# A fused Fourier-mixing and two-product kernel: the second product runs three rounds behind the first, and the transform's pieces get two places in a round

## The chip, the cores and the metric

One core of a Trainium2 chip runs the whole program. TensorE (PE in the profile, with its weight loads as PEld), VectorE (DVE), ScalarE (ACT), GpSimd (POOL) and SyncE (SP, which issues the transfers here) each work through a list of their own in order and wait for each other by semaphores. The metric is the device time in microseconds (us) of one execution of the program.

## The reference

Eight sequences of 3008 tokens and 256 features pass through a real Fourier transform along the sequence, a complex 256x256 mix with a bias and a soft threshold, and the inverse transform. The result, 24064 rows of 256, goes through a block of two products with 2048 hidden features, whose nonlinearity is the square of a relu.

```python
X = np.fft.rfft(x, axis=1); Xr, Xi = X.real, X.imag
Yr = Xr @ w_r - Xi @ w_i + b_r
Yi = Xr @ w_i + Xi @ w_r + b_i
Yr, Yi = (np.sign(v) * np.maximum(np.abs(v) - 0.01, 0.0) for v in (Yr, Yi))
y = np.fft.irfft(Yr + 1j * Yi, n=3008, axis=1)      # x of the second part, 24064 x 256
h = np.maximum(y @ w_in, 0.0)                       # 24064 x 2048
out = h * h @ w_out                                 # 24064 x 256
```

## The kernel before

A start-up part loads the weights, splits them into a high and a low fp32r part and transforms the first sequences. After it the program is a loop of rounds, written out by hand (L904): 47 chunks of 512 tokens, eight rounds a chunk, 376 rounds and the two that empty the pipe. Round r does the following for its chunk.

- The **first product** (`mm1`, tile `ph`, 12 matmuls of 512 columns) for 256 hidden features. ScalarE takes it out of PSUM (relu L863, square L864), VectorE makes three sums of it (`sums`, L869 to L871).
- The hidden tile of the round before is split: ScalarE copies the high part `gh` (L916), VectorE subtracts the low part `gl` (L927).
- The **second product** (`mm2`, tile `po`, 14 matmuls with `gh` and 7 with `gl`, 256 columns each) for the hidden tile of `LAG` = 2 rounds before. It adds up in four PSUM banks over eight rounds; in the round of a chunk's last one `put_together` reads them (one ScalarE copy, seven VectorE operations L890 to L896) and stores the result. This round is called the chunk end below.

Between these the transform of later sequences is threaded in, one piece at a time. Each piece is a few matmuls into one bank of `ps_f`, a pool of two PSUM banks that are given out in turn: a piece takes the bank that the piece but one before it had, and waits until that one has been read.

- Piece A (`psa`, 6 matmuls of 256 columns), first step of the transform of a group of columns; ScalarE copies it out (`eva`). Before it come `f` (VectorE), `fh` (ScalarE), `fl` (VectorE).
- A pair B: `psb` (8 small matmuls; ScalarE reads it into `x`, VectorE sums, both split it to `xh`, `xl`); two rounds later the mix `psm`, 18 matmuls into two banks at once, which VectorE reads one after the other (`e`, L233 and L234) and thresholds (`t`, L727, and `e`, L728); then ScalarE turns it (`z`), both split it (`zh`, `zl`), and `psc` (3 matmuls of 512 columns) goes back; ScalarE copies it out (`evc`).
- Piece D (`psd`, 8 small matmuls), last step; ScalarE copies half of it (`dv`, L784), VectorE combines it with the other half (`dx`, L275 and L276), which frees the bank; then it is split into `xt`, the operand of the first product.

Where a step stands is set by a place in the round: `load`, `p1` (pieces behind the first product), `e` (ScalarE, behind the square), `p2` (behind the second product), `a` and `v` (ScalarE and VectorE, last in the round). `PAIR_WORK` and the others are guesses of PE, ScalarE and VectorE time, by which `spread` chooses the rounds of pieces A and D; `pair_rounds` fixes those of the pairs. In this text rounds count from 0 and a chunk end before has r mod 8 = 1.

Of the kernel before, what the change touches and what calls it, by code (L numbers as in the profile page):

```python
# [20 lines left out]
NPAIR = NR // 2  # L21
# [128 lines left out]
def fft_mix_moe(ctx: ExitStack, tc: tile.TileContext, xp, xu, w_r, w_i, b_r, b_i,  # L150
# [473 lines left out]

    rounds = pair_rounds(B)
    last = nch * NU
    plan = {}
    works = np.zeros((last + 64, 3))
# [14 lines left out]
    A_WORK = ((-3, 0, 0, .8), (-2, 0, .6, .7), (0, .7, .6, 0))  # L643
    D_WORK = ((0, .9, .4, .8), (1, 0, .7, .7))
    SUM_WORK = (0, 0, .3, 2.9)

    def plan_a(b, i, r):
# [38 lines left out]
        at(r, "p1", points)  # L686
        at(r, "e", out)

    def plan_b(b, i, r):
# [82 lines left out]
    def plan_d(i, r, later):  # L772
# [16 lines left out]

        at(r - 1, "load", load)  # L790
        at(r, "p1", points)
        at(r, "e", take)
        at(r, "v", unfolded)
        for n, piece in enumerate(pieces(i)):
            q = later if n else r + 1
            at(q, "a", lambda piece=piece: high_x(piece, s["x"]))
            at(q, "v", lambda piece=piece: low_x(piece, s["x"]))

    for b, rs in rounds.items():
        for r in rs:  # L800
            note(r, *PAIR_WORK)
    for c in range(nch):
        works[c * NU + NU + 1] += SUM_WORK[1:]

    mixes = {r + 2 for rs in rounds.values() for r in rs}
    def spread(n, lo, hi, work, apart):

        best = [{} for _ in range(n)]
        for i in range(n):
            for r in range(lo, hi + 1):  # L810
                if r in mixes:
                    continue
                cost = sum(max(0., float(np.sum(works[r + d] + w))) ** 2 - float(np.sum(works[r + d])) ** 2
                           for d, *w in work)
                before = min(((c, q) for q, (c, _) in best[i - 1].items() if q <= r - apart),
                             default=None) if i else (0., ())
                if before is not None:
                    best[i][r] = before[0] + cost, (best[i - 1][before[1]][1] if i else ()) + (r,)
        got = min(best[-1].values())[1]
        for r in got:  # L820
            note(r, *work)
        return got

    begin = 3
    for b in range(2, B):
        end = rounds[b][0] - 3
        got = spread(len(GROUPS), begin, end, A_WORK, 2)
        begin = max(got[-1] + 2, rounds[b][0] - 12)
        for i, r in enumerate(got):
            plan_a(b, i, r)  # L830
# [6 lines left out]
    free = 2  # L837
    for c in range(1, nch):
        own = [i for i in range(len(flat)) if begins[i] // CH == c]
        parts = [[i for i in own if flat[i][0] == b] for b in sorted({flat[i][0] for i in own})]  # L840
        for n, part in enumerate(parts):
            b = flat[part[0]][0]
            lo = max(NU * (c - 1), free, rounds[b][-1] + 9 if b else 2)
# [128 lines left out]
```

## Time and profile before

| what | value |
|---|---|
| median of 3 runs (lowest to highest) | 2706.86 us (2706.52 to 2708.56) |
| the profiled execution | 2706.33 us, of it span of the trace 2704.2 us |
| PE, PEld busy | 2580.7 us (95%), 2288.4 us (85%) |
| DVE, ACT busy | 2112.6 us (78%), 1982.9 us (73%) |
| granted TensorE clock, mean | 0.99 |
| DMA, mean over the span | 61 GB/s |

Busy time is the time that an engine had an instruction in work, as a share of the span. A matmul's end is modelled: a matmul of 512 columns is shown 0.39 us long while the next one starts 0.23 us after it, so a wait of TensorE shows shorter in the busy time than from one start to the next. The first matmul of round 2 starts at 155.13 us.

### The profile page before, as it was taken

How to read it: one execution, taken by the hardware profiler on the slowest of the kernel's cores; microseconds unless marked ns; L12 is line 12 of the kernel's file. 1: busy time of each engine (PE TensorE's matmuls, PEld its weight loads, DVE VectorE, ACT ScalarE, POOL GpSimd, SP SyncE). 2: the span in 40 equal slices, each digit the busy share in tenths (PEclk: the TensorE clock that was granted, in tenths of full speed). 3: DMA queues.
4: the chain of work that ended last, by engine and by line, in shares of the span. 5: the costliest groups of instructions: out<-in, count | busy, mean ns of one | idle time of the engine just before them, and what ended most of it. 6: DMA issues, size and time to landing. Idle time of an engine off the chain costs nothing.

```text
span 2704.2 us, 41768 instructions
## 1 busy us (share of the span) xinstructions
PE 2580.7 (95%) x16496; PEld 2288.4 (85%) x16496; DVE 2112.6 (78%) x3155; ACT 1982.9 (73%) x2764; POOL 48.2 (2%) x57
## 2 busy tenths in 40 slices
PE   7889999999999999999999999999999999999998
PEld 4578888888888889888888888888888998888887
DVE  5777887877788878877888788887887778777776
ACT  4667776767777777777787777877777777776766
POOL 1500000000000000000000000000000000000000
PEclk8999999999999999999999999999999999999999
DMA  8522222211112111121112111211111111001000
GB/s 261 182 67 65 65 65 69 65 50 60 56 57 69 57 57 56 60 65 46 56 60 68 54 57 53 75 53 51 57 56 48 38 39 51 31 24 35 16 27 16
DMA packets 113092, 164.57 MB, mean 61 GB/s; under 512 B 9584, under 2 KB 63074, under 8 KB 112706
## 3 DMA queue, kind: packets, MB, share of 16 engines
q1 hardware_dynamic: 112898, 161.91, 19.3%
q8 instruction: 131, 2.15, 0.3%
q14 instruction: 63, 0.52, 0.1%
HBM read 86.90 MB, written 74.97 MB: 60 GB/s over the span
## 4 chain that ended last, share of the span: by engine, by line
PE 72%; ACT 11%; DVE 7%; issue 7%; DMA 1%; SPq 0%; DVEq 0%; ACTq 0%
PE po L878 17%; PE ph L184 10%; PE ph L182 10%; PE ph L183 10%; PE po L882 9%; ACT gh L916 4%; ACT g L863 4%; PE psd L268 3%; PE psm L184 2%; PE psm L182 2%; PE psm L183 2%; PE psb L219 1%; DVE gl L927 1%; PE psc L182 1%; ACT x L223 1%
## 5 line engine op out<-in xcount | busy, mean ns | idle before, releaser
L927 DVE TENSOR_TENSOR gl<-g,gh 128x1792 fp32r<-128x1792 f32 x376 | 761.2, 2025 | 144.2 <-ACT gh L916 144.1
L863 ACT ACTIVATE g<-ph 128x512 f32<-128x512 f32 x752 | 408.4, 595 | 592.0 <-PE ph L184 590.9
L878 PE MATMUL po<-gh,wo 128*128 128x256 f32 x5264 | 703.6, 284 | 29.2 <-DVE o L891 17.9
L878 PEld LDWEIGHTS po<-gh,wo 128*128 128x128 f32 x5264 | 657.9, 189 | 57.5 <-DVE o L895 16.7
L916 ACT CAST gh<-g 128x1792 fp32r<-128x1792 f32 x376 | 636.2, 1692 | 0.2 <-DVE g L871 0.2
L182 PE MATMUL ph<-xt,wi 128*128 128x512 f32 x1504 | 592.7, 394 | 10.1 <-DVE dx L276 8.8
L184 PE MATMUL ph<-xt,wi 128*128 128x512 f32 x1504 | 591.1, 393 | 0.0
L183 PE MATMUL ph<-xt,wi 128*128 128x512 f32 x1504 | 590.7, 393 | 0.0
L869 DVE TENSOR_TENSOR g<-g 128x512 f32<-128x512 f32 x376 | 259.9, 691 | 332.7 <-ACT g L864 331.6
L864 ACT ACTIVATE g<-g 128x1024 f32<-128x1024 f32 x376 | 398.9, 1061 | 11.9
L882 PE MATMUL po<-gl,wo 128*128 128x256 f32 x2632 | 369.1, 280 | 0.2 <-DVE gl L927 0.2
L184 PEld LDWEIGHTS ph<-xt,wi 128*128 128x128 f32 x1504 | 283.3, 188 | 64.6
L882 PEld LDWEIGHTS po<-gl,wo 128*128 128x128 f32 x2632 | 334.9, 188 | 0.4 <-DVE gl L927 0.4
L182 PEld LDWEIGHTS ph<-xt,wi 128*128 128x128 f32 x1504 | 283.5, 188 | 59.0 <-ACT xt L280 9.0
L183 PEld LDWEIGHTS ph<-xt,wi 128*128 128x128 f32 x1504 | 283.2, 188 | 47.9
L871 DVE TENSOR_TENSOR g<-g 128x256 f32<-128x256 f32 x376 | 159.9, 425 | 12.9
L870 DVE TENSOR_TENSOR g<-g 128x256 f32<-128x256 f32 x376 | 160.0, 425 | 12.8
L184 PE MATMUL psm<-wm,xl 128*128 128x256 f32 (+1 forms) x552 | 162.3, 294 | 0.7 <-DVE xl L712 0.6
L182 PE MATMUL psm<-wm,xh 128*128 128x256 f32 (+1 forms) x552 | 162.1, 294 | 0.3 <-ACT x L223 0.3
L183 PE MATMUL psm<-wm,xh 128*128 128x256 f32 (+1 forms) x552 | 159.9, 290 | 0.0
L268 PEld LDWEIGHTS psd<-tD,din 120*128 120x128 f32 (+1 forms) x832 | 105.7, 195 | 50.5 <-ACT g L863 30.5
L268 PE MATMUL psd<-tD,din 120*128 120x120 f32 (+1 forms) x832 | 117.2, 285 | 32.2 <-ACT g L863 25.5
(102 smaller groups left out, 2572.4 us busy)
## 6 DMA issues: line engine op xcount, KB each, us to landing
bin<-s SPq DMA_DIRECT2D x96, 256.0 KB
s<-evc SPq DMA_DIRECT2D x96, 256.0 KB
outT_dram<-o SPq DMA_DIRECT2D x94, 256.0 KB
din<-s SPq DMA_DIRECT2D x96, 240.0 KB
xin<-in_xp_dram SPq DMA_DIRECT2D x72, 240.0 KB
s<-eva SPq DMA_DIRECT2D x72, 240.0 KB
s<-eva SPq DMA_DIRECT2D x22, 192.0 KB
w<-in_moe_w_in_dram SPq DMA_DIRECT2D x8, 512.0 KB
```

The lines of the kernel that those rows point to most:

```text
L182: nc.tensor.matmul(out, l0, r0, start=start, stop=False, **kw)
L183: nc.tensor.matmul(out, l0, r1, start=False, stop=False, **kw)
L184: nc.tensor.matmul(out, l1, r0, start=False, stop=stop, **kw)
L268: nc.tensor.matmul(ps[:, k, part], t[:n, s:s + P], tD[:n, tab + part, :n], start=True, stop=True)
L863: nc.scalar.activation(g[:, 2 * a:2 * a + 2], ph[:, a].rearrange("p (t m) -> p t m", t=2), AF.Relu)
L864: nc.scalar.activation(g[:, 0:4], g[:, 0:4], AF.Square)
L869: nc.vector.tensor_sub(g[:, 4:6], g[:, 1:4:2], g[:, 0:2])
L870: nc.vector.tensor_sub(g[:, 6], g[:, 3], g[:, 4])
L878: nc.tensor.matmul(out, wo_[k][j][:, s], gh[:, s], start=j == 0 and half == 0 and k == 0, stop=False, skip_group_check=True)
L882: nc.tensor.matmul(out, wo_[0][j][:, s], gl[:, s], start=False, stop=j == NU - 1, skip_group_check=True)
L916: nc.scalar.copy(split_[k][0], hid[k])
L927: nc.vector.tensor_sub(gl, hid.pop(r - 1), gh.bitcast(F32))
```

## The change

The second product of a hidden tile comes three rounds behind the first (`LAG` 3 for 2; `gh` and `gl` keep two buffers each), so a chunk end now has r mod 8 = 2. Pieces A and D get a place `p`: `p1` or the new use of `p2` right behind the second product, at most one piece in each place of a round; `psb` stays in `p1`, the mix and `psc` are in `p2`. There are four new reading places: `e` and `e2` (ScalarE, VectorE) for what `p1` made, `f` and `f2` for `p2`. `e2` is ahead of `gl`; in a chunk end `put_together` goes ahead of `gh` and `gl`. A pair's steps are closer together (split of x in its own round, threshold with the mix, turn one round earlier, `psc` at r+5 or r+6 for r+7). The calendar is new: pairs every second round for sequences 1 and 2 and every third after them, before every second or third and then every fourth.

```diff
 def pair_rounds(nb):
 
-    out = {1: [1, 3, 5, 7, 9, 11, 13, 15, 17, 19, 22, 25]}
+    out = {1: [1 + 2 * i for i in range(NPAIR)]}
     for b in range(2, nb):
-        last = 25 + 48 * (b - 1)
-        out[b] = [last - (3 if b == 2 else 4) * (NPAIR - 1 - i) for i in range(NPAIR)]
+        last = 23 + 48 * (b - 1)
+        out[b] = [last - (2 if b == 2 else 3) * (NPAIR - 1 - i) for i in range(NPAIR)]
...
+    LAG = 3
...
-    PAIR_WORK = ((0, .9, .6, .4), (1, 0, .8, 1.), (2, 2.1, 0, 1.4), (3, 0, 0, 1.1), (4, 0, 1.8, 0),
-                 (5, 0, .6, .7), (7, .7, .6, 0))
...
+    PAIR_WORK = ((0, .6, .4), (1, .8, 1.), (2, 0, 2.5), (3, 1.8, 0), (4, .6, .7), (6, .6, 0))
+    BACK = {b: 5 + (b > 2) for b in range(1, B)}
+    A_WORK = ((-3, 0, .8), (-2, .6, .7), (0, .6, 0))
+    D_WORK = ((0, 1., 1.5),)
+    SUM_WORK = ((1, .3, 2.9),)
+
+    EVAC = {"p1": ("e", "e2"), "p2": ("f", "f2")}
+
...
-        at(r, "p1", points)
-        at(r, "e", out)
+        at(r, p, points)
+        at(r, EVAC[p][0], out)
...
         at(r - 1, "load", load)
         at(r, "p1", points)
         at(r, "e", take)
-        at(r, "v", lambda: sum_x(s["x"]))
-        at(r + 1, "a", high)
-        at(r + 1, "v", low)
+        at(r, "e2", lambda: sum_x(s["x"]))
+        at(r, "f", high)
+        at(r, "v", low)
         at(r + 2, "p2", mix)
-        at(r + 2, "v", biased)
-        at(r + 3, "v", threshold)
-        at(r + 4, "a", turned)
-        at(r + 5, "a", zhigh)
-        at(r + 5, "v", zlow)
-        at(r + 7, "p1", back)
-        at(r + 7, "e", out)
+        at(r + 2, "f2", biased)
+        at(r + 2, "v", threshold)
+        at(r + 3, "a", turned)
+        at(r + 4, "a", zhigh)
+        at(r + 4, "v", zlow)
+        at(r + BACK[b], "p2", back)
+        at(r + BACK[b], "f", out)
...
         at(r - 1, "load", load)
-        at(r, "p1", points)
-        at(r, "e", take)
-        at(r, "v", unfolded)
+        at(r, p, points)
+        at(r, act, take)
+        at(r, dve, unfolded)
...
+            q, act, dve = (later, "e", "e2") if n else (r, "a", "v") if p == "p1" else (r + 1, "e", "e2")
...
+
+    taken = set()
+    mixes = set()
     for b, rs in rounds.items():
         for r in rs:
             note(r, *PAIR_WORK)
+            mixes.add(r + 2)
+            use = {(r, 0), (r + 2, 1), (r + BACK[b], 1)}
+            assert not use & taken
+            taken |= use
...
+    def spread(n, lo, hi, work, apart, beside):
+
+        slots = [(r, h) for r in range(lo, hi + 1) for h in range(2)
+                 if (r, h) not in taken]
...
-            for r in range(lo, hi + 1):
-                if r in mixes:
-                    continue
+            for r, h in slots:
+                cost = .3 * h + .3 * ((r, 1 - h) in taken) + beside * (r in mixes) + sum(
+                    float(np.sum((works[r + d] + w) ** 2 - works[r + d] ** 2)) for d, *w in work)
+                before = min(((c, q) for q, (c, _) in best[i - 1].items() if q[0] <= r - apart),
...
-    LAG = 2
     with tc.manual_schedule():
         for r in range(last + LAG):
             c, j = divmod(r, NU)
...
             run(r, "p1")
             run(r, "e")
-            k = r - 1
-            if k in hid:
-                split_[k] = opnd("gh", F32R, 2), opnd("gl", F32R, 2)
-                nc.scalar.copy(split_[k][0], hid[k])
             k = r - LAG
+            cc, jj = divmod(k, NU)
+            ends = k >= 0 and jj == NU - 1
+
+            def high():
+                if r - 1 in hid:
+                    split_[r - 1] = opnd("gh", F32R, 2), opnd("gl", F32R, 2)
+                    nc.scalar.copy(split_[r - 1][0], hid[r - 1])
+
+            def low():
+                if r - 1 in hid:
+                    gh, gl = split_[r - 1]
+                    nc.vector.tensor_sub(gl, hid.pop(r - 1), gh.bitcast(F32))
+
+            if not ends:
+                high()
             if k >= 0:
-                cc, jj = divmod(k, NU)
                 if jj == 0:
                     pos[cc] = [ps_o.tile([P, 512], F32, tag=f"o{i}", name=f"po{i}") for i in range(4)]
                 mm2(jj, pos[cc], *split_.pop(k))
+            run(r, "p2")
             if r < last:
-                sums(g)
-            if r - 1 in hid:
-                gh, gl = split_[r - 1]
-                nc.vector.tensor_sub(gl, hid.pop(r - 1), gh.bitcast(F32))
-            run(r, "p2")
-            if k >= 0 and jj == NU - 1:
+                sums(hid[r])
+            run(r, "e2")
+            if ends:
                 put_together(cc, pos.pop(cc))
+                high()
+            else:
+                low()
+            run(r, "f")
+            run(r, "f2")
+            if ends:
+                low()
             run(r, "a")
```

VectorE, before, rounds 100 and 101, from the split `gl` of round 100 to that of round 101 (`dx<-psd` is the reading of a D piece, `g<-g` the sums):

```order
L927 TENSOR_TENSOR gl<-g,gh 128x1792 [waits Activation_49]
L668 TENSOR_TENSOR fl<-f,fh 120x512 [waits Activation_49]
L727 TENSOR_SCALAR t<-e 128x512
L728 TENSOR_TENSOR e<-e,t 128x512 [waits DVE_49]
L275 TENSOR_TENSOR dx<-psd,dv 128x2x120 [waits PE_49]
L276 TENSOR_TENSOR dx<-psd,dv 128x2x115
L869 TENSOR_TENSOR g<-g 128x512 [waits Activation_49]
L870 TENSOR_TENSOR g<-g 128x256 [waits DVE_49]
L871 TENSOR_TENSOR g<-g 128x256 [waits DVE_49]
L927 TENSOR_TENSOR gl<-g,gh 128x1792 [waits PE_49,Activation_49]
```

Here the reading of round 100's `psd` is the round's last work.

VectorE, now, round 117, which also holds a D piece, from the sums to the last split:

```order
L882 TENSOR_TENSOR g<-g 128x512 [waits Activation_49]
L883 TENSOR_TENSOR g<-g 128x256 [waits DVE_49]
L884 TENSOR_TENSOR g<-g 128x256 [waits DVE_49]
L275 TENSOR_TENSOR dx<-psd,dv 128x2x120 [waits Activation_49]
L276 TENSOR_TENSOR dx<-psd,dv 128x2x115
L936 TENSOR_TENSOR gl<-g,gh 128x1792 [waits PE_49,Activation_49]
L748 TENSOR_TENSOR zl<-z,zh 128x512 [waits Activation_49]
L285 TENSOR_TENSOR xt_9234<-dx,xt_9233 128x2x61 [waits Activation_49]
```

The reading of `psd` went from the end of the round, behind `gl`, `fl` and the threshold, to ahead of `gl`.

VectorE, before, the chunk end of round 105, from the last sum to the next round's first (`o<-po` are `put_together`):

```order
L871 TENSOR_TENSOR g<-g 128x256 [waits DVE_49]
L927 TENSOR_TENSOR gl<-g,gh 128x1792 [waits PE_49,Activation_49]
L890 TENSOR_TENSOR o_8884<-po_8373,o_8884 128x256 [waits DMAHW5_49,PE_49,Activation_49]
L891 TENSOR_TENSOR o_8884<-po_8372,o_8884 128x256 [waits DVE_49]
L892 TENSOR_TENSOR o_8885<-po_8373,o_8884 128x256
L893 TENSOR_TENSOR o_8884<-po_8374,o_8884 128x256 [waits DVE_49,PE_49]
L894 TENSOR_TENSOR o_8885<-po_8374,o_8885 128x256
L895 TENSOR_TENSOR o_8884<-po_8374,o_8884 128x256 [waits DVE_49]
L896 TENSOR_TENSOR o_8885<-o_8885,po_8375 128x256 [waits DVE_49,PE_49]
L227 TENSOR_TENSOR x<-x 128x256
L869 TENSOR_TENSOR g<-g 128x512 [waits Activation_49]
```

There the seven operations that free the `po` banks stand behind `gl`.

VectorE, now, the chunk end of round 114 from the fifth of the seven on, and round 115 up to the reading of the first bank of its mix (`e<-psm`):

```order
L907 TENSOR_TENSOR o_9421<-po_8902,o_9421 128x256
L908 TENSOR_TENSOR o_9420<-po_8902,o_9420 128x256 [waits DVE_49]
L909 TENSOR_TENSOR o_9421<-o_9421,po_8903 128x256 [waits DVE_49,PE_49]
L936 TENSOR_TENSOR gl<-g,gh 128x1792 [waits Activation_49]
L748 TENSOR_TENSOR zl<-z,zh 128x512 [waits Activation_49]
L285 TENSOR_TENSOR xt_9234<-dx,xt_9233 128x2x235 [waits Activation_49]
L882 TENSOR_TENSOR g<-g 128x512 [waits Activation_49]
L883 TENSOR_TENSOR g<-g 128x256 [waits DVE_49]
L884 TENSOR_TENSOR g<-g 128x256 [waits DVE_49]
L936 TENSOR_TENSOR gl<-g,gh 128x1792 [waits PE_49,Activation_49]
L233 TENSOR_TENSOR e<-psm_9501,bias_68 128x512 [waits PE_49]
```

The seven (now L903 to L909) went ahead of `gl`; `gl` and the splits `zl` and `xt` now stand between them and the next round's sums, and with them ahead of the mix's reading.

## Rows read from the trace of the kernel before

**Rows 1.** Windows: stretch, length, busy of PE, PEld, DVE, ACT, POOL; clock, DMA share, GB/s.
```profile
145.00:350.00 205.00, 197.44 (x1272) 177.61 (x1273) 164.70 (x254) 157.61 (x229) 2.11 (x1) 0.97 0.20 62
```

**Rows 2.** Timeline of PE (start, length): first matmuls of rounds 2, 77, 321, 375.
```profile
155.13 0.50 PE L182 MATMUL ph<-xt,wi 128*128 128x512 f32 x1
...
717.23 0.40 PE L182 MATMUL ph<-xt,wi 128*128 128x512 f32 x1
...
2380.28 0.39 PE L182 MATMUL ph<-xt,wi 128*128 128x512 f32 x1
...
2685.92 0.39 PE L182 MATMUL ph<-xt,wi 128*128 128x512 f32 x1
```

**Rows 3.** Chain of waits in order of time (start, us to the next piece, what).
```profile
439.43 0.89 PE psb L219 x8
440.32 0.89 PE psd L268 x8
441.21 1.64 PE po L878 x14
...
2586.51 0.23 PE ph L182
```

**Rows 4.** Waits of PE from 145 us on: who for whom, total us, times, longest.
```profile
PE psd L268 <- ACT g L863: 25.5, 26, 1.3
PE po L878 <- DVE o L891: 17.9, 31, 1.6
PE psa L182 <- DVE e L233: 12.6, 9, 3.9
...
PE po L878 <- DVE o L895: 8.1, 32, 0.3
```

**Rows 5.** Timeline, round 101: a pair's first piece and a D piece; brackets: idle before.
```profile
887.67 1.06 PE L219 MATMUL psb<-tB,bin 128*128 128x128 f32 x8
887.87 1.09 ACT L863 ACTIVATE g<-ph 128x512 f32<-128x512 f32 x2 [2.03 <-PE ph L184]
...
889.28 0.39 DVE L276 TENSOR_TENSOR dx<-psd,dv 128x230 f32<-128x230 f32 x1
889.77 1.12 PE L268 MATMUL psd<-tD,din 120*128 120x120 f32 x8 [1.05 <-ACT g L863]
...
890.07 0.69 DVE L869 TENSOR_TENSOR g<-g 128x512 f32<-128x512 f32 x1 [0.40 <-ACT g L864]
...
891.26 0.43 DVE L871 TENSOR_TENSOR g<-g 128x256 f32<-128x256 f32 x1
```

**Rows 6.** Timeline of DVE at one chunk end.
```profile
1030.25 2.03 DVE L927 TENSOR_TENSOR gl<-g,gh 128x1792 fp32r<-128x1792 f32 x1 [0.41 <-ACT gh L916]
1032.20 0.42 DVE L890 TENSOR_TENSOR o<-po,o 128x256 f32<-128x256 f32 x1
...
1034.51 0.41 DVE L896 TENSOR_TENSOR o<-o,po 128x256 f32<-128x256 f32 x1
```

**Rows 7.** Groups by line: count, then busy us, mean ns; idle before.
```profile
L737 ACT ACTIVATE z<-e,sg 64x256 f32<-64x256 f32 x168 | 85.2, 507 | 2.1
...
L736 ACT COPY z<-e 64x256 f32<-64x256 f32 x168 | 68.0, 405 | 1.0
...
L745 DVE TENSOR_TENSOR zl<-z,zh 128x512 fp32r<-128x512 f32 x84 | 57.5, 684 | 0.0
L233 DVE TENSOR_TENSOR e<-psm,bias 128x512 f32<-128x512 f32 x84 | 57.4, 683 | 0.0
...
L285 DVE TENSOR_TENSOR xt<-dx,xt 128x470 fp32r<-128x470 f32 x52 | 33.6, 645 | 1.6 <-ACT xt L280 1.6
```

**Rows 8.** Timeline of PE after a wait.
```profile
219.82 0.38 PE L182 MATMUL psa<-fh,tAs 120*120 120x256 f32 x1 [1.88 <-DVE e L233]
...
220.81 0.63 PE L182 MATMUL psc<-zh,tMs 128*128 128x512 f32 x1
```

**Rows 9.** Timeline of PE, last second product: its end.
```profile
2697.32 0.98 PE L882 MATMUL po<-gl,wo 128*128 128x256 f32 x7
```

More of the change, by code (lines that the diff above doesn't have):

```diff
@@ L627, in fft_mix_moe @@
     plan = {}
-    works = np.zeros((last + 64, 3))
+    works = np.zeros((last + 64, 2))
     def at(r, place, do):
@@ L788, in unfolded @@
             unfold(i, s["ps"], s["v"], s["x"])
+        act, dve = EVAC[p]
         at(r - 1, "load", load)
-        at(r, "p1", points)
-        at(r, "e", take)
-        at(r, "v", unfolded)
+        at(r, p, points)
+        at(r, act, take)
+        at(r, dve, unfolded)
         for n, piece in enumerate(pieces(i)):
-            q = later if n else r + 1
-            at(q, "a", lambda piece=piece: high_x(piece, s["x"]))
-            at(q, "v", lambda piece=piece: low_x(piece, s["x"]))
+            q, act, dve = (later, "e", "e2") if n else (r, "a", "v") if p == "p1" else (r + 1, "e", "e2")
+            at(q, act, lambda piece=piece: high_x(piece, s["x"]))
+            at(q, dve, lambda piece=piece: low_x(piece, s["x"]))
+    taken = set()
+    mixes = set()
     for b, rs in rounds.items():
@@ L801, in fft_mix_moe, with plan_all_a @@
             note(r, *PAIR_WORK)
+            mixes.add(r + 2)
+            use = {(r, 0), (r + 2, 1), (r + BACK[b], 1)}
+            assert not use & taken
+            taken |= use
     for c in range(nch):
-        works[c * NU + NU + 1] += SUM_WORK[1:]
-    mixes = {r + 2 for rs in rounds.values() for r in rs}
-    def spread(n, lo, hi, work, apart):
+        note(c * NU + NU + LAG - 2, *SUM_WORK)
+    def spread(n, lo, hi, work, apart, beside):
+        slots = [(r, h) for r in range(lo, hi + 1) for h in range(2)
+                 if (r, h) not in taken]
         best = [{} for _ in range(n)]
         for i in range(n):
-            for r in range(lo, hi + 1):
-                if r in mixes:
-                    continue
-                cost = sum(max(0., float(np.sum(works[r + d] + w))) ** 2 - float(np.sum(works[r + d])) ** 2
-                           for d, *w in work)
-                before = min(((c, q) for q, (c, _) in best[i - 1].items() if q <= r - apart),
+            for r, h in slots:
+                cost = .3 * h + .3 * ((r, 1 - h) in taken) + beside * (r in mixes) + sum(
+                    float(np.sum((works[r + d] + w) ** 2 - works[r + d] ** 2)) for d, *w in work)
+                before = min(((c, q) for q, (c, _) in best[i - 1].items() if q[0] <= r - apart),
                              default=None) if i else (0., ())
                 if before is not None:
-                    best[i][r] = before[0] + cost, (best[i - 1][before[1]][1] if i else ()) + (r,)
+                    best[i][r, h] = before[0] + cost, (best[i - 1][before[1]][1] if i else ()) + ((r, h),)
         got = min(best[-1].values())[1]
-        for r in got:
+        taken.update(got)
+        for r, _ in got:
             note(r, *work)
[L822 to L830, printed above, removed]
+        return [(r, f"p{h + 1}") for r, h in got]
+    def plan_all_a(b, begin):
+        got = spread(len(GROUPS), begin, rounds[b][0] - 3, A_WORK, 2, 0)
+        for i, rp in enumerate(got):
+            plan_a(b, i, *rp)
+        return max(got[-1][0] + 2, rounds[b][0] - 12)
     for b, rs in rounds.items():
@@ L836, in fft_mix_moe @@
         at(0, "v", lambda i=i, xf=xf: low_x(pieces(i)[1], xf))
-    free = 2
+    free, begin, b = 2, 3, 2
     for c in range(1, nch):
+        while b < B and rounds[b][0] <= NU * c:
+            begin = plan_all_a(b, begin)
+            b += 1
         own = [i for i in range(len(flat)) if begins[i] // CH == c]
@@ L841, in fft_mix_moe @@
         for n, part in enumerate(parts):
-            b = flat[part[0]][0]
-            lo = max(NU * (c - 1), free, rounds[b][-1] + 9 if b else 2)
-            got = spread(len(part), lo, NU * c - 3 - sum(map(len, parts[n + 1:])), D_WORK, 1)
-            free = got[-1] + 1
-            for i, r in zip(part, got):
-                plan_d(i, r, NU * c)
+            at_b = flat[part[0]][0]
+            lo = max(NU * (c - 1), free, rounds[at_b][-1] + BACK[at_b] + 3 if at_b else 2)
+            got = spread(len(part), lo, NU * c - 3 - sum(map(len, parts[n + 1:])), D_WORK, 1, 20)
+            free = got[-1][0] + 1
+            for i, rp in zip(part, got):
+                plan_d(i, *rp, NU * c)
     def mm1(c, j):
```

10 lines of the change are left out of this document (3 added, 7 removed).

## The prediction

> **What bounds the kernel now.** I read three views: the timeline of TensorE from one first product to the next, the chain of waits for what a piece costs, and TensorE's waits. The first product has a matmul every 0.23 us, the second one every 1.64/14 = 0.117 us [rows 3], so a round without a transform piece is 12 x 0.23 + 21 x 0.117 = 5.22 us. A piece adds: `psb` or `psd` 0.89 [rows 3], `psa` 6 x 0.117 = 0.70, a mix 18 x 0.117 = 2.11, `psc` 3 x 0.23 = 0.69. With these prices, and the pieces that stand in each stretch of the program, I compare what the stretches take [rows 2] with what they would take if TensorE never waited:
>
> - rounds 2 to 76: 562.1 us; 75 rounds, 23 `psb`, 21 `psd`, 26 `psa`, 24 mixes, 22 `psc` make 514.7; lost 47.4.
> - rounds 77 to 320: 1663.1 us; 244 rounds, 60, 67, 52, 60, 62 make 1592.5; lost 70.6.
> - rounds 321 to 374: 305.6 us; 54 rounds and 13 `psd` make 293.5; lost 12.2.
> - the tail: first product 2.76, then three second products of 2.46 from 2685.92 make 2696.1; the last seven matmuls start at 2697.32 and take 7 x 0.117 = 0.82, to 2698.1 [rows 2, 3, 9]; lost 2.1.
>
> So TensorE bounds the loop, and 132.3 us is all that an order can give back. Nothing in the change touches the start (155.1 us [rows 2]) or the few us behind the last matmul.
>
> The waits have three kinds [rows 4]. A D piece waits for its bank (25.5 us, 26 times). The row names ScalarE's relu, but the timeline shows that relu long begun, and `psd` starting 0.1 us behind the end of `dx` (889.28 + 0.39 = 889.67; 889.77) [rows 5]: the bank is the one of the D piece before, whose reading stands last on VectorE. The second product waits at chunk ends for `put_together` (17.9 + 8.1 us). A `psa` waits for the reading of a mix (12.6 us, up to 3.9). A 256-column matmul is shown 0.28 us long but gives way after 0.117, so each wait is some 0.16 longer than its row says, and the shorter ones have no row: these three kinds and their kin fill the 132.
>
> **The change part by part.** No instruction is added or removed: the pieces of the stretches above are the same within a few, and TensorE's sum without waits changes by under 2 us.
>
> *The D piece alone in its place, its reading ahead of `gl`.* In the order shown for round 117 the bank is read right behind the sums, and the next piece with this bank comes at least two pieces later. Reading by the sums' end plus 0.8 (two `dx`) is done before the second product of the same round ends; what waited 25.5 us plus 26 x 0.16 = 30 us waits no more. A D piece in `p2` followed by one in `p1` of the next round leaves its transfer only the first product's 2.76 us. This stands at two places; I charge 1 us each, 2 in all.
>
> *`put_together` ahead of `gl`.* It takes 1034.92 - 1032.20 = 2.7 us [rows 6]. Behind `gl` (2.03) it ended after the next round's second product was due. Ahead of it, it starts with the sums' end or the second product's end, some 6.5 us into a round that lasts at least 5.2, and ends near 9.5; the next second product starts at 5.2 + 2.8 = 8.0 or later and reaches the banks one by one over 1.6 us, the first read 0.8 us into the seven. So 26.0 plus 63 x 0.16 = 36 us goes. What is late now is `gl`, 2.7 us later, and everything behind it on VectorE, a strict list: `zl`, `xt`, then the next round's sums, its `gl` and the reading of a mix.
>
> *That is the new wait.* Round 114, then 115 (`psa`, mix), then 116 with `psb`, whose bank is the first of the mix. From the start of round 114: first product to 2.76, relu 0.2 later, square done 2.2 behind the relu's start [rows 5]. The turn of round 113 (2 x 0.405 + 2 x 0.507 = 1.8 [rows 7]) can hold the relu up by 0 to 1.8; I take 1.5. Square done at 6.65, sums 1.6 [rows 5] to 8.25, `dx` 0.8 to 9.05, `put_together` 2.7 to 11.75, `gl` 2.03 to 13.8, `zl` 0.69 and `xt` 0.65 [rows 7] to 15.1; then round 115's sums to 16.7, `gl` to 18.7, first reading of the mix 0.68 to 19.4. Round 115 starts at 5.22 + 0.89 = 6.1 and lasts 5.22 + 0.70 + 2.11 = 8.0; `psb` could start at 6.1 + 8.0 + 2.76 = 16.9. It waits 2.5 us (1.0 without the late relu, 3.2 without the `psa`). In the calendar of rounds 77 to 320 such a chunk end (a round before a mix) comes twice in each of five sequences: 10 x 2.3 = 23. Chunk ends in the round of a `psb` or of a mix push the same reading by less, 0.5 to 1.2 by the same steps: 10 x 0.9 = 9. The sequences' last chunk ends have no mix behind them: 0. Together 32 us, where the bounds are 0 and 10 x 3.2 + 10 x 1.2 = 44.
>
> *The same chain without a chunk end.* Less 2.7, the last reading but one ends at 16.7 against 16.9, or 16.1 against 16.2 in rounds with no `psa` (where the relu is less late). That margin of 0.2 holds or not by errors of mine: bounds 0 and 84 x 0.5 = 42 us; I take 6.
>
> *The dense stretch, rounds 2 to 76.* Sequence 1 had its pairs every second round already, and there VectorE was busy 164.7 of 205 us [rows 1], 80%: it has time to catch up, and the chunk ends among these pairs now hold no `p1` piece but one. I leave 5 of 47 us.
>
> *`LAG` 3 with two buffers.* `gh` is now written in the round in which the second product still reads the tile two before it, so ScalarE waits for those 14 matmuls. They end at 2.76 + 1.64 + the `p1` piece (0 to 0.9) = 4.4 to 5.3; ScalarE gets there at 5.1 (relu and square) plus the reading of that piece. Hidden: 0, and it costs a few tenths of ScalarE's slack if not. In the tail one more second product stands between the last first product and its own second one; it covers the wait for the last `gh` and `gl`: 2.1 us gained.
>
> *The clock.* Behind a wait of 1.88 us the next 512-column matmul is shown at 0.63 us and not 0.40, half the speed [rows 8]; the granted clock of the stretch around it is 0.97 [rows 1]. Behind the waits of 1.05 us it shows nothing (eight `psd` matmuls in 1.12) [rows 5]. New waits of 1 to 3 us lie between: of 10 I let half cost 0.8. That is 4 us, with bounds 0 and 8. [...]
>
> **Sum.** Lost now 132.3; stays: 32 + 6 + 5 + 2 + 4 = 49. Gain 83. The profiled execution took 2706.33 us with a span of 2704.2, 0.5 under the median of 2706.86, so 2706.3 - 83 = 2623 us.
>
> **The rivals.**
> 1. *No new wait.* If the relu is not late and the slack at chunk ends is larger than I count, VectorE catches up: the 32, 6 and 4 go too, gain 125, 2581 us. For it: VectorE is busy 80% where the pairs are closest [rows 1], and my chain adds full lengths where neighbours overlap by 0.1. Against: VectorE's list is strict and 15.1 us of it stands in 14.1 us of TensorE. 14%.
> 2. *Every pair waits.* The margin of 0.2 fails and `psb` waits 0.5 in each of 84 pairs: 36 more than I charge, 2659 us. For: it is one late operation away, and pairs every third round leave less room than every fourth. Against: a wait of TensorE gives VectorE the same time back. 20%.
> 3. *Slower.* The same place, but the chain is late by far more: ScalarE, held by the new wait of `gh` behind the second product, hands on relu, `gh` and turn late in each round of a pair. From 83/84 = 1.0 us per pair above my count it eats the gain; at 1.3 us the time is 2623 + 84 x 1.3 = 2732. Against: `gh` is needed two rounds later, and its wait ends before ScalarE gets there. 6%.
> 4. *The places change nothing.* Banks are still given in turn from two, a mix takes both; if what was seen as a wait for `dx` is mostly one for the piece's own neighbour, the waits move with it: 2706. Against: in the order shown the reading is 2 us or more earlier. 2%.
>
> **How the numbers follow.** Forecast 58%, with its own range 2604 to 2646 (the new waits between 13 and 44, the margin between 0 and 20). Rivals 14, 20, 6 and 2%. The range reaches down to 2590, half way into rival 1, and up to 2660, over rival 2. Within 0.2% (5.4 us, about what can be told from no change) lies rival 4 and the low edge of rival 3: 3%. Slower 6%, faster 91%.
>
> **What the changed profile would show.** Right: no `psd` waits for VectorE or ScalarE, `po` waits near 0, `psb` waits for `e` (L233) behind chunk ends, 1 to 3 us each; rounds without chunk end at 5.22 plus their pieces. Wrong: `psb` waits in most pairs (rival 2), or TensorE waits for `gl` or ScalarE idles before `gh` for more than 0.3 us (rival 3). If no `psb` waits at all, my chain on VectorE was too long.

## The result and the profile after

The changed kernel takes 2602.68 us (2601.37 to 2607.08, 4 runs) where the kernel before, on the same chip, takes 2707.22 (2706.52 to 2708.56, 4 runs). The ratio is 0.9616, with a 95% interval of 0.9599 to 0.9633: 104.5 us faster. The prediction had 83 us and 2623; the measured time lies 1.3 us under the forecast's own range (2604 to 2646) and half way between 2623 and rival 1's 2581. The profiled execution took 2602.41 us, with a span of 2600.6, which is 103.6 less than before.

The first lines of the page of the changed kernel: span; then busy time, share of the span and instructions.

```profile
span 2600.6 us, 41936 instructions
...
PE 2540.9 (98%) x16496; PEld 2281.6 (88%) x16496; DVE 2106.6 (81%) x3155; ACT 1993.3 (77%) x2764; POOL 48.1 (2%) x57
```

The three stretches are read as in [rows 2], from the first matmuls of rounds 2, 77, 321 and 375. This is the timeline of TensorE (start, length, what).

```profile
155.23 0.50 PE L182 MATMUL ph<-xt,wi 128*128 128x512 f32 x1 [0.28 <-ACT g L876]
...
669.48 0.39 PE L182 MATMUL ph<-xt,wi 128*128 128x512 f32 x1
...
2287.38 0.40 PE L182 MATMUL ph<-xt,wi 128*128 128x512 f32 x1
...
2582.05 0.39 PE L182 MATMUL ph<-xt,wi 128*128 128x512 f32 x1
...
2593.80 0.98 PE L895 MATMUL po<-gl,wo 128*128 128x256 f32 x7
```

With the prediction's prices and the pieces that now stand in each stretch (23 `psb`, 21 `psd`, 22 `psa`, 24 mixes, 24 `psc`; then 60, 68, 56, 60, 60; then 12 `psd`), TensorE without waits needs 513.3, 1594.8 and 292.6 us. It took 514.3, 1617.9 and 294.7, so it lost 1.0, 23.1 and 2.1. In the tail it lost nothing: 2582.05 + 2.76 + 4 x 2.46 = 2594.65, and the last seven matmuls start at 2593.80 and take 0.82. One correction to that sum: round 2 has no second product now (the first comes in round 3, and the tail has one more), so the time lost in rounds 2 to 76 is 2.5 more, 3.5. That makes 132.3 lost before and 28.7 now; the difference, 103.6, is the whole change of the span. By stretch, 47.4 became 3.5, 70.6 became 23.1, 12.2 became 2.1, and the 2.1 of the tail went.

TensorE's waits from 145 us on in the changed kernel (who for whom, total us, times, longest), to be set against [rows 4]:

```profile
...
PE psb L219 <- DVE e L233: 5.3, 10, 0.8
PE psd L268 <- DMA din<-s: 4.1, 5, 1.6
PE psm L182 <- DVE dx L276: 3.1, 4, 0.9
PE ph L182 <- ACT g L876: 2.5, 3, 1.2
PE po L891 <- DVE o L908: 0.8, 3, 0.3
...
PE po L891 <- DVE o L904: 0.2, 1, 0.2
```

The 25.5 us of `psd` and the 26.0 of the second product are gone. The wait that the prediction put in their place, `psb` for the reading `e` of a mix, is there, at ten places and at most 0.8 us long, where it had 1 to 3 us each. This is one of the ten, round 114 (a chunk end) to round 116, in the timeline of three engines (brackets: idle before):

```profile
914.10 0.40 PE L182 MATMUL ph<-xt,wi 128*128 128x512 f32 x1
...
918.02 1.08 ACT L876 ACTIVATE g<-ph 128x512 f32<-128x512 f32 x2
...
920.23 0.69 DVE L882 TENSOR_TENSOR g<-g 128x512 f32<-128x512 f32 x1 [1.39 <-ACT g L877]
...
922.38 0.41 DVE L903 TENSOR_TENSOR o<-po,o 128x256 f32<-128x256 f32 x1
...
925.02 2.02 DVE L936 TENSOR_TENSOR gl<-g,gh 128x1792 fp32r<-128x1792 f32 x1
926.95 0.68 DVE L748 TENSOR_TENSOR zl<-z,zh 128x512 fp32r<-128x512 f32 x1
927.56 0.64 DVE L285 TENSOR_TENSOR xt<-dx,xt 128x470 fp32r<-128x470 f32 x1
...
929.64 2.02 DVE L936 TENSOR_TENSOR gl<-g,gh 128x1792 fp32r<-128x1792 f32 x1
931.57 0.68 DVE L233 TENSOR_TENSOR e<-psm,bias 128x512 f32<-128x512 f32 x1
932.31 1.16 PE L219 MATMUL psb<-tB,bin 128*128 128x128 f32 x8 [0.79 <-DVE e L233]
933.22 1.88 PE L891 MATMUL po<-gh,wo 128*128 128x256 f32 x14
```

It is the predicted chain step by step: relu, sums, `put_together`, `gl`, `zl` and `xt`, the next round's sums and `gl`, then the mix, and 0.06 us behind its end (932.25) the `psb`. VectorE has no gap of over 0.11 us from 920.23 to there. Only it runs faster than forecast: its last link ends 18.15 us into round 114 and not 19.4.

### The profile page after: what moved, and what is told of

Same layout as the page of the kernel before. It is cut to its first block, busy times and chain, and to the rows that moved or that the text cites. A ratio compares the mean times of both kernels' runs of the same rounds, so it can differ in the third digit from the quotient of the medians.

```text
span 2600.6 us, 41936 instructions
## 1 busy us (share of the span) xinstructions
PE 2540.9 (98%) x16496; PEld 2281.6 (88%) x16496; DVE 2106.6 (81%) x3155; ACT 1993.3 (77%) x2764; POOL 48.1 (2%) x57
## 4 chain that ended last, share of the span: by engine, by line
PE 84%; DVE 7%; ACT 5%; DMA 2%; issue 1%; SPq 0%; DVEq 0%; ACTq 0%
PE po L891 21%; PE ph L182 12%; PE ph L184 12%; PE ph L183 12%; PE po L895 10%; PE psd L268 3%; PE psb L219 3%; PE psm L182 2%; PE psm L184 2%; PE psm L183 2%; DVE gl L936 2%; ACT g L876 1%; ACT g L877 1%; DMA din<-s 1%; DVE g L882 1%
## 5 line engine op out<-in xcount | busy, mean ns | idle before, releaser
L876 ACT ACTIVATE g<-ph 128x512 f32<-128x512 f32 x752 | 409.1, 596 | 458.0 <-PE ph L184 456.5
L891 PE MATMUL po<-gh,wo 128*128 128x256 f32 x5264 | 695.2, 282 | 1.6 <-DVE o L908 0.8
L931 ACT CAST gh<-g 128x1792 fp32r<-128x1792 f32 x376 | 638.2, 1697 | 17.2 <-PE po L891 13.6
L219 PEld LDWEIGHTS psb<-tB,bin 128*128 128x128 f32 x768 | 101.1, 194 | 35.4 <-issue 17.4
```

The costliest lines, as they stand in the source:

```text
L219: nc.tensor.matmul(ps[:, k, :, q, :], tv[:, q, k], tB[:, 0:r + 2:r + 1], start=True, stop=True)
L876: nc.scalar.activation(g[:, 2 * a:2 * a + 2], ph[:, a].rearrange("p (t m) -> p t m", t=2), AF.Relu)
L891: nc.tensor.matmul(out, wo_[k][j][:, s], gh[:, s], start=j == 0 and half == 0 and k == 0, stop=False, skip_group_check=True)
L931: nc.scalar.copy(split_[r - 1][0], hid[r - 1])
```

## The experiments

The times are medians of 4 runs where nothing else is said; each ratio is to the kernel before on the same chip, with a 95% interval. The heading of each says which of the two kernels it edits. The kernels ran on several chips, where the kernel before took 2705.8 to 2707.4 us, so a difference of one or two us between edited kernels means nothing. "Start to start" is a matmul's distance to the next one less what that distance is without a wait.

**`put_together` behind `gl` again, in the changed kernel.**

```
-            if ends: put_together(cc, pos.pop(cc)); high()
-            else: low()
+            low()
             run(r, "f"); run(r, "f2")
-            if ends: low()
+            if ends: put_together(cc, pos.pop(cc))
```

(`high()` stands ahead of the second product in every round then, so the chunk end's copy out of `po` is behind `gh` on ScalarE again too.)

> The changed kernel (2602.7 us) with one part undone: at a chunk end `put_together` stands behind `gl` again, second product still three rounds behind. Theory A, the move of `put_together` by itself pays for the waits that were 42 us in the kernel before (first products to `po`, counted from start to start): they come back, 25 to 45 us, so 2628 to 2648. Theory B, the other parts already hide it: within 6 us of 2603.

Measured: 2664.19 us, ratio 0.9841 (0.9826 to 0.9856), 61.5 above the changed kernel, more than either theory had. TensorE's waits:

```profile
PE po L891 <- DVE o L904: 36.3, 31, 2.1
...
PE po L891 <- DVE o L908: 7.3, 40, 0.2
```

The old wait returns, longer than in [rows 4] (17.9 us, up to 1.6). Start to start, 15 rounds lose 27.1 us between the first product and the second, 1.8 each. Part of the 61.5 is the clock: the granted clock was 0.50 in four stretches of 3.4 us, and in none in the changed kernel; by half of these 13.7 us it is at most 7 (an estimate).

**`LAG` 2 in the changed kernel.** One line, `LAG = 2`. It does not move the second product alone: the weights by which `spread` places pieces A and D know the chunk ends, and in over 100 of the 376 rounds these pieces stand elsewhere.

> The changed kernel with the second product two rounds behind, all else as it is (`put_together` ahead of `gl`). Theory A, the lag pays only in the tail (2.1 us in my sum): 2604 to 2608. Theory B, the lag is what lets `put_together` stand first: in the changed trace `gl` of a chunk end ends 12.9 us after the round's start, and with a lag of two the next round's seven last matmuls, due some 10 to 11 us after that start, would wait for it, 1 to 2.5 us at 46 chunk ends: 2645 to 2715.

Measured: 2616.21 us, 0.9662 (0.9648 to 0.9677), 13.5 slower than with 3. It lies between the two theories. The wait is the one of theory B, with a smaller total:

```profile
PE po L895 <- DVE gl L936: 17.8, 24, 1.3
```

So `LAG` 3, with the pieces that it moves, is worth more than the tail: with `put_together` ahead, `gl` at a chunk end is late for a second product two rounds behind the first, and not for one three rounds behind. In return the ten waits of `psb` for `e` are not there with `LAG` 2; the 13.5 us are the balance.

**Both: `LAG` 2 and `put_together` behind `gl`.** The two edits above in one kernel.

> The changed kernel with both undone: lag of two and `put_together` behind `gl`. If the two parts are independent (A), its loss is the sum of the losses of the two kernels that undo one each. If the lag only serves the earlier `put_together` (B), it takes the time of the kernel that undoes the put alone, within 6 us, and less than the lag of two alone.

Measured: 2641.27 us, 0.9756 (0.9741 to 0.9770), 38.6 above changed, where the two edits alone cost 61.5 + 13.5 = 75.

```profile
PE po L891 <- DVE o L904: 21.8, 30, 1.9
PE po L891 <- DVE o L908: 9.2, 39, 0.6
```

Neither theory holds; the two interact. `put_together` ahead is worth 61.5 us at `LAG` 3 and 2641.3 - 2616.2 = 25.1 at 2; `LAG` 3 is worth 13.5 with it ahead and costs 2664.2 - 2641.3 = 22.9 with it behind. Neither number belongs to one edit, and the moved pieces are in both comparisons across the lag.

**`put_together` ahead of `gl`, alone, in the kernel before.**

```
             if r < last: sums(g)
+            if k >= 0 and jj == NU - 1: put_together(cc, pos.pop(cc))
             if r - 1 in hid:
                 ...
             run(r, "p2")
-            if k >= 0 and jj == NU - 1: put_together(cc, pos.pop(cc))
```

> The kernel before (2707 us), lag of two, old calendar, with one part of the change alone: `put_together` ahead of `gl` at chunk ends. Theory A, the move by itself is worth the `po` waits, 36 us by my prediction: 2665 to 2680. Theory B, at a lag of two it trades the wait for the banks for one for `gl`: within 15 us of 2707, and TensorE's waits name `gl` (L923 or so) in place of `o`.

Measured: 2702.21 us (10 runs), 0.9982 (0.9972 to 0.9991).

```profile
PE po L882 <- DVE gl L929: 30.2, 32, 1.3
PE psd L268 <- ACT g L863: 25.8, 26, 1.3
```

The 26.0 us of the second product's wait for `put_together` [rows 4] turn into 30.2 for `gl`, at 32 chunk ends. Theory B holds. In this kernel `gh` also stays ahead of the chunk end's first copy out of `po` on ScalarE, where the changed kernel has the copy first. So it is the move on VectorE alone.

**The D piece's bank read behind `gl` again, in the changed kernel.** `high_x` and `low_x` of its first part move with it, to the next round.

```
-        at(r, dve, unfolded)
+        at(r, "v", unfolded)
...
-            ... (r, "a", "v") if p == "p1" else (r + 1, "e", "e2")
+            ... (r + 1, "a", "v")
```

> The changed kernel with the reading of every D piece (`dx`) back at the end of the round, behind `gl`; the pieces stay where they are. Theory A (my prediction), reading ahead of `gl` is what ends the waits of `psd`: some 30 us come back, 2625 to 2640. Theory B, a place of its own is what ends them, since the next piece with the same bank now comes a round later whatever the reading's place: within 8 us of 2603.

Measured: 2614.23 us, 0.9661 (0.9646 to 0.9675), 11.5 slower. The D pieces don't wait for it; mixes do:

```profile
PE psm L182 <- DVE e L233: 13.0, 4, 3.6
```

It is nearer to theory B. With two places the next D piece does not come to the bank before it is read, early or late. What pays are the four rounds (109, 145, 256, 301) in which a mix follows a `psd` of `p1`: between the two parts of the mix 3.1 to 3.8 us are lost start to start. The other bank still holds the `psd` there, so the second part waits for the reading `e` of the first: in round 109 it starts at 888.12, when `e` ends at 888.06, and `dx` begins only at 892.80.

**One place for all pieces but the mix, in the changed kernel.** `psa`, `psc` and `psd` that stood in `p2` go to `p1` of the same round.

```
-        at(r, p, points)
-        at(r, EVAC[p][0], out)
+        at(r, "p1", points)
+        at(r, "e", out)
```

> The changed kernel with all pieces but the mix in the place behind the first product again (A, D and `psc` that stood behind the second product go ahead of it, read at the first reading places); same rounds, same order of everything else. Theory A, the second place is worth little once the reading is early: within 8 us of 2603. Theory B, two pieces side by side meet banks that were not yet read (the second reading of a mix comes 0.7 us after the first): 0.5 us or more at each `psc`, 82 of them, 2640 or more.

Measured: 2619.30 us, 0.9681 (0.9666 to 0.9695), 16.6 slower, between the theories.

```profile
PE psc L183 <- DVE zl L748: 8.4, 16, 1.2
PE psc L182 <- DVE e L233: 5.3, 10, 0.8
```

`psc` now stands ahead of the second product, some 2.5 us earlier, and waits for its own input `zl`; and it has taken over the ten waits of `psb` for `e`. That is what the second place is worth on the new calendar; of the loss, 14.9 us start to start are in rounds 2 to 76, where the pairs are closest. The `psd` waits of the old one end without it, as the next run shows.

**The D piece's bank read ahead of `gl`, alone, in the kernel before.**

```
-        at(r, "v", unfolded)
+        at(r, "e2", unfolded)
...
                 sums(g)
+            run(r, "e2")
```

(The first part's `high_x` and `low_x` go to `a` and `v` of round r, those of a second part to `e` and `e2` of theirs.)

> The kernel before with one part alone: every D piece read by VectorE behind the sums, ahead of `gl` (and its split in the same round). Lag, places and calendar as they were. Theory A, this ends the waits of `psd` (25.5 us and 26 times 0.16, 30 us): 2672 to 2682. Theory B, with two pieces in one place the wait goes over to ScalarE's reading of the piece before: within 12 us of 2707.

Measured: 2677.96 us, 0.9897 (0.9882 to 0.9911), 28 faster: theory A, against the 30 that the prediction had.

```profile
PE po L878 <- DVE o L891: 19.2, 32, 1.6
```

The `psd` wait of 25.5 us [rows 4] is gone and the others stand as they were. The relu that the row names was indeed not the releaser, since it stands where it stood.

**`put_together` ahead and `LAG` 3, in the kernel before.** The edit shown for the first of these and `LAG = 3`.

> The kernel before with two parts of the change together: lag of three and `put_together` ahead of `gl`; old calendar, all pieces but the mix in one place, D pieces read last. At a lag of two the same move only gained 4.6 us, its waits for the banks turned into waits for `gl`. Theory A, with the third round of lag neither wait is left: 36 to 42 us under 2706.5, 2664 to 2671. Theory B, the 2.7 us that now stand ahead of everything on VectorE at a chunk end make the readings of D pieces and mixes late, and half or more comes back: 2680 or more.

Measured: 2786.73 us, 1.0295 (1.0280 to 1.0310): 80 us slower. Theory A (2664 to 2671) falls. Theory B (2680 or more) had the direction and not the size, and what is late most is a split, `xl`, and not a reading. Three views: TensorE's waits,

```profile
PE psm L184 <- DVE xl L712: 58.9, 36, 2.3
PE psd L268 <- ACT g L864: 35.7, 21, 1.9
```

ScalarE's waits,

```profile
ACT gh L916 <- PE po L878: 80.3, 91, 2.6
```

and the timeline of one round of a pair:

```profile
952.86 1.70 ACT L916 CAST gh<-g 128x1792 fp32r<-128x1792 f32 x1 [0.34 <-PE po L878]
954.46 0.36 ACT L889 COPY o<-po 128x256 f32<-128x256 f32 x1
...
954.85 0.43 DVE L890 TENSOR_TENSOR o<-po,o 128x256 f32<-128x256 f32 x1 [1.43 <-ACT o L889]
...
957.50 2.02 DVE L929 TENSOR_TENSOR gl<-g,gh 128x1792 fp32r<-128x1792 f32 x1
959.44 0.68 DVE L745 TENSOR_TENSOR zl<-z,zh 128x512 fp32r<-128x512 f32 x1
960.04 0.95 DVE L712 TENSOR_TENSOR xl<-x,xh 128x768 fp32r<-128x768 f32 x1
...
961.04 0.39 PE L184 MATMUL psm<-wm,xl 128*128 128x256 f32 x1 [1.69 <-DVE xl L712]
```

Here `gh` waits 0.34 us for the second product, which stands late because two pieces (`psa`, `psd`) stand ahead of it; the copy out of `po` stands behind `gh`, `put_together` waits 1.43 us for the copy, and `xl`, last on VectorE, ends 2 us after the mix has begun. The wait of `gh` does not decide this. Eight rounds later, with one piece ahead of the second product, `gh` does not wait, and the mix waits for `xl` as long:

```profile
1010.52 1.70 ACT L916 CAST gh<-g 128x1792 fp32r<-128x1792 f32 x1
...
1018.71 0.38 PE L184 MATMUL psm<-wm,xl 128*128 128x256 f32 x1 [1.71 <-DVE xl L712]
```

Of the 36 waits, 33 lie in rounds with r mod 8 = 3, and nearly all of these are 1.7 us long, whether `gh` waited 0, 0.1 or 0.3 us. What they share is the place: `LAG` 3 moves the chunk end from r mod 8 = 1, the round of a `psb`, to 2, the round at whose end the old calendar splits that pair's x for the mix of the next round. Of the 80.3 us of `gh` only 7.0 stand in chunk ends. The same kernel with `LAG` 2 takes 2702.2, so the larger lag costs 84.5 us on this calendar, of which the mix's new wait for `xl` has 58.9 in its row. The granted clock has a share too: 0.50 in eleven stretches of 3.4 us, against one of 6.8 us with `LAG` 2, which by half of the difference is at most 15 us (an estimate). What the waits of `gh`, the prediction's third rival, cost here isn't shown.

**All three, in the kernel before.** The D piece's reading ahead, `put_together` ahead, `LAG` 3; the calendar, the one place and the place of the split of x as before.

> As the last, and D pieces read ahead of `gl`: three parts on the old calendar. If the parts add (28 us for the reading alone, and what the last kernel gains), its time is the last kernel's less 28 us, within 6. What it then lacks to the changed kernel's 2602.7 is the worth of the second place and the new calendar together: by theory A of the last 30 to 40 us, with `psa` waiting for the reading of a mix as the main row left.

Measured: 2719.40 us, 1.0046 (1.0029 to 1.0062), still 12 slower than before.

```profile
PE psm L184 <- DVE xl L712: 63.8, 38, 2.1
```

The `psd` waits for ScalarE's square are off the list, and `gh` still waits 59.5 us in total. The parts do not add: the reading ahead gains 67 us here and 28 alone. What remains of the change, taken together, is worth 2719.4 - 2602.7 = 117 us on top of these three parts: the second place, x split in the pair's own round, the copy out of `po` ahead of `gh`, the new calendar. In these four kernels that start from the one before the copy stays behind `gh`. VectorE's wait for it is 1.5 us in all in the kernel before, 30.3 with `put_together` ahead at `LAG` 2, 49.1 at `LAG` 3 and 32.3 in this one. How much of their loss is this alone wasn't tried, and neither was x split in the pair's own round, which would take `xl` out of the chunk end's round; so the 117 us, where 30 to 40 were expected, are not divided among the four parts.

**The new wait taken away by distance.** In the changed kernel, pairs every fourth round in sequences 4 to 7.

```
-        out[b] = [last - (2 if b == 2 else 3) * (NPAIR - 1 - i) ...]
+        out[b] = [last - (2 if b == 2 else 3 if b == 3 else 4) * (NPAIR - 1 - i) ...]
-    BACK = {b: 5 + (b > 2) ...}
+    BACK = {b: 5 + 2 * (b == 3) ...}
```

> The changed kernel with pairs every fourth round in sequences 4 to 7, as before, in place of every third (`psc` five rounds behind `psb` there, seven in sequence 3). Theory A, the loop is now bound by TensorE's own work and the calendar's density is worth little: within 8 us of 2603. Theory B, the closer pairs are a gain of their own: 2618 or more. Theory C, sparser pairs have fewer waits for the mix's reading (6.9 us of `psb` waits now): 2597 or less.

Measured: 2593.61 us, 0.9585 (0.9569 to 0.9601), 9 faster than the changed kernel: theory C.

```profile
PE psd L268 <- DMA din<-s: 4.8, 6, 0.9
...
PE psb L219 <- DVE e L233: 0.2, 1, 0.2
```

**The new wait taken away by order.** In the changed kernel, in the round behind a chunk end that holds a mix, VectorE reads the mix ahead of `gl`.

```
+            after_end = k >= NU and jj == 0 and r in mixes
...
-            else: low()
+            elif not after_end: low()
             run(r, "f"); run(r, "f2")
-            if ends: low()
+            if ends or after_end: low()
```

> The changed kernel, but in the round behind a chunk end, where it holds a mix, VectorE reads the mix ahead of `gl`. Theory A, the ten waits of `psb` behind chunk ends (6.9 us from start to start) come from `gl` in front of that reading, 2.0 us long: they go, 2594 to 2598. Theory B, the late relu and sums set them: 2601 to 2604. If `gl` two rounds later becomes late, slower than 2604.

Measured: 2593.99 us, 0.9588 (0.9575 to 0.9601), 8.7 faster: theory A.

```profile
PE psm L182 <- DVE dx L276: 3.1, 4, 0.9
```

The line of `psb` and `e` is gone from TensorE's waits. Here all pieces stand where they stood, and rounds 77 to 320 take 9.0 us less (1608.9 for 1617.9), of which the waits themselves are 6.9 start to start: the order alone takes the wait away. That the sparser pairs also gave 9 us is chance: there the calendar moved pieces in over 200 rounds, and beside the waits of `psb` (6.5 us start to start) those of mixes for `dx` (3.8) and of the second product in rounds 77 to 320 went, while `psd` waits 5.2 us longer. These two kernels beat both others; the two edits weren't tried together.

**The same, and the D pieces' transfers given more time.** By the rule, a D piece may not follow one in `p2` of the round before, and the first of a sequence comes a round later.

```
-    if q[0] <= r - apart
+    if q[0] <= r - apart - (beside > 0 and q[1] > h)
-    rounds[at_b][-1] + BACK[at_b] + 3
+    rounds[at_b][-1] + BACK[at_b] + 4
```

> As the kernel that reads the mix ahead of `gl` behind a chunk end, and the first D piece of a sequence one round later behind its last `psc`, and no D piece in the first place right behind one in the second, where the calendar's rule reaches. Theory A, the waits of `psd` for its transfer (5.2 us from start to start in the changed kernel, seven of them) shrink: 2 to 4 us under that kernel. Theory B, they move with the piece: no difference.

Measured: 2595.13 us (5 runs), 0.9587 (0.9574 to 0.9600): no difference to the kernel that only reads the mix first.

```profile
PE psd L268 <- DMA din<-s: 3.6, 5, 1.5
```

This is no test of either theory: the edit moved one D piece, from round 320 to 323. The pieces of rounds 180 and 228 still stand in `p1` right behind one in `p2`, and wait 1.5 and 1.6 us start to start, about as before. What would end these waits (5.1 us start to start in the changed kernel) stays open.

## Why the prediction was right, point by point

**What bounds the kernel.** Right: TensorE's sum without waits holds before and after, and the lost time explains the change of the span to 0.1 us. But not all that was lost before were waits, as the point on the clock shows.

**The new waits at chunk ends: the term that was mis-sized, 32 us forecast and 6.9 measured.** The mechanism and the places are right: the ten places are exactly those ten where a chunk end comes in a round before a mix. Start to start, the five whose chunk end holds a `psd` (114, 162, 210, 258, 306) lose 0.95 to 0.98 us and the other five (90, 138, 186, 234, 282) 0.39 to 0.43, against 2.3 forecast. The other ten chunk ends lose nothing, against 0.9. The chain was 1.25 us too long: the relu came 3.92 us into the round, 1.16 behind the first product's 2.76, where the prediction took 0.2 + 1.5 = 1.7, so 0.5 of it was the relu. The rest is that neighbours on VectorE overlap by some 0.1 (the `zl` behind the first `gl` shown starts at 926.95, and `gl` ends at 927.04), as the prediction's first rival held. TensorE's side of the difference was 17.25 us and not 16.9. Taking the wait away by order alone is worth 9 us.

**The margin of 0.2 us in every pair: 6 forecast, 0 measured.** The same shorter chain gives the margin room: outside the ten places no `psb` waits.

**The dense stretch: 5 forecast, 3.5 measured.** The 44 us gained here (some 6 of them the clock's, see below) are two fifths of the whole, and the reason given, that VectorE has time to catch up, prices no part of the change. Most of it is not traced to a part: these rounds, which lose 47.4 us in the kernel before, lose 47.6 with the D piece's reading ahead, 45.3 with `put_together` ahead and 57.9 with all three; in the changed kernel giving up the second place costs 14.9 here. VectorE is busy 173.39 of 205 us there (164.70 before [rows 1]), and no `psb` waits for it (in the window's row the granted clock stands behind the five engines):

```profile
145.00:350.00 205.00, 201.86 (x1327) 183.48 (x1328) 173.39 (x261) 168.21 (x244) 2.10 (x1) 0.99 0.18 59
```

**The transfer: 2 forecast, 5.1 measured** in rounds 77 to 320, at 6 places and not 2; two of them (rounds 180 and 228, 1.5 and 1.75 us) are those with a `p2` piece followed by one in `p1`.

**What was not forecast.** A mix waits for `dx` where it shares a round with a `psd` of `p1` (3.8 us, 4 places). The second product's small waits for banks behind chunk ends are 3.5 us in rounds 77 to 320 and 2.1 in rounds 321 to 374, where 0 was forecast. The prediction had let `put_together` end near 9.5 us into the round in one place and at 11.75 in another; in round 114 it ended at 11.0, 1.4 us behind the start of the next second product.

**The clock: 4 forecast, 0 measured, and a gain that was not forecast.** The `psb` that waited 0.79 us is eight matmuls long, shown as 1.16, and the second product behind it starts 933.22 - 932.31 = 0.91 later, the full speed's 0.89 within 0.02. No run shows the 0.8 us that the prediction charged for a new wait: the granted clock of the changed kernel is 1.00 from 150 to 2590 us. In the kernel before it was 0.50 in three stretches of rounds 2 to 76, the first of them 0.6 us behind the wait of [rows 8]:

```profile
220.40:223.80 3.40, 3.40 (x16) 3.09 (x15) 1.95 (x5) 1.17 (x2) 0.00 (x0) 0.50 0.63 195
285.25:288.65 3.40, 3.40 (x14) 3.11 (x15) 2.40 (x5) 0.99 (x3) 0.00 (x0) 0.50 0.71 249
572.00:578.75 6.75, 4.97 (x23) 4.98 (x24) 3.86 (x8) 1.26 (x3) 0.00 (x0) 0.50 0.44 152
```

TensorE was busy 11.8 us there, and half of that, some 6 us (an estimate), is what the clock took of the 132.3. In the changed kernel no such stretch is left.

**Reading the D bank ahead of `gl`: 30 forecast.** Right where it was measured alone, on the old calendar (28). On the new calendar it is worth 11.5, since two places already part the banks.

**`put_together` ahead of `gl`: 36 forecast. `LAG` 3: nothing but 2.1 in the tail.** The sum of the two came out right by luck (38.1 forecast, 38.6 with both undone), for the parts were wrong. Alone on the old calendar the first gives 5 us: "what is late now is `gl`" was seen, but who waits for it was looked for among the pairs and not in the second product two rounds behind. `LAG` 3 is what takes that wait away. In the changed kernel, with the pieces that the lag moves, the first is worth 61.5 and the second 13.5, and without the other they are worth 25.1 and less than nothing.

**`gh` with two buffers and `LAG` 3: "hidden".** Right in the changed kernel for the time, though a sign that the prediction named for rival 3, ScalarE idle before `gh` for more than 0.3 us, did show (ScalarE's waits):

```profile
ACT g L876 <- PE ph L184: 456.5, 266, 4.6
...
ACT gh L931 <- PE po L891: 13.6, 21, 1.3
```

Only 21 of 376 `gh` wait, 0.65 us each in the mean and 13.6 in all, against 456.5 in which ScalarE waits for the first product anyway. That is not a property of `LAG`: the prediction's working took at most one piece (0 to 0.9 us) ahead of the second product, and where two stand there, in the old calendar, the same two buffers wait 91 times, 80.3 us. Rival 3's wait exists there, but the largest loss of that kernel, the mix's wait for `xl`, does not come from it.

So the forecast held in what goes and in where the new wait stands. It was 20 us too high mostly because one chain of 18 us was counted 1.25 us too long, beside 17 us of TensorE. That its three priced parts make the gain is not shown: on the old calendar they lose 12 us together. Together they pay only with the rest of the change, to which the prediction gave no price, and how the gain divides stays open.

## What to carry to other kernels

Where an engine's strict list is nearly as long as the bound engine's work, the wait is the difference of two large sums: 1.25 us of error in a chain of 18 made the term nearly five times too large, so price each link at its start-to-start distance and give the range to the difference. A step moved ahead in such a list needs a second look at who waits for what it pushed back, and in which round: here the next one was the second product, and in the changed kernel the larger lag ended it. A larger lag also moves the chunk end by a round against a calendar that stays: on the old one into the round that splits x for the next round's mix, where the lag cost 84.5 us with 58.9 in the row of that wait, while on the one laid out for it the lag was worth 13.5. And parts that are priced one by one may pay only together.

## What the runs showed of the hardware

Where a VectorE operation does not wait for the one ahead, it starts before that one is shown to end: `zl` 0.09 us before the end of a `gl` of 2.02, `xt` 0.07 before that of `zl`. Where it does wait for it, as in the sums, it starts 0.03 to 0.04 behind its end (920.96 behind 920.92). Behind a wait the first matmul gives way 0.10 us later, and the following ones keep their distance: behind 0.79 us the second `psb` matmul starts after 0.21 instead of 0.11, and behind 1.69 us, in the kernel with `LAG` 3 on the old calendar, the 256-column matmul at 961.04, whose weights are loaded from 961.04 on too, is shown as 0.39 instead of 0.28, and the next starts 0.22 later and not 0.117. The granted clock is 1.00 around both, so this is not the clock. Waits of one length do not all lower it: of that kernel's 32 waits of a mix for `xl` of 1.7 us, four were followed within 1.6 us by a stretch of 3.4 us at 0.50, the others were not.
